# Two DFT steps joined by one SBUF-to-SBUF transfer per slot instead of a trip through a DRAM scratch, with the first chunk put in a new order

## The chip, the cores and the metric

The kernel runs on one core of a Trainium2 chip. The metric is the device time of one execution in microseconds, the median of several runs. The engines named below are PE (TensorE, matrix products), DVE (VectorE), ACT (ScalarE), POOL (GpSimd) and SP (SyncE, which here only issues DMAs). Each engine works through its own instructions in a fixed order.

## The reference

For each of 8 batches a 3136 x 256 input goes through a two-dimensional Fourier transform, of which the real part is kept. A normalised MLP with a residual follows.

```python
X = np.fft.fft(x, axis=1); X = np.fft.fft(X, axis=2); x = X.real      # x: 8 x 3136 x 256
mu = np.mean(x, axis=-1, keepdims=True)
var = np.mean((x - mu) ** 2, axis=-1, keepdims=True)
xn = (x - mu) / np.sqrt(var + 1e-06) * g_ln
ch = np.maximum(xn @ w_ch1, 0.0) @ w_ch2                              # 256 -> 1024 -> 256
return x + ch
```

The two weight matrices arrive as 64-bit floats.

## The kernel before, in words

**The transform.** The DFT of length 3136 is split into 64 x 49. `step1(b, i)` does the transforms of length 64 for batch `b` and one of 7 input tiles `i`. Each tile holds two of the 14 slots (`NS`). The result is copied by ACT into the SBUF tile `s1` (128 partitions, 14 slots, 256 values), and `step1_ends` adds the last column of each slot. `step2(m, ...)` does the second step for one of 64 pieces `m`, eight to a batch: part "m" is its matmuls, which contract over 112 partitions of `s2` (`KP`, 8 rows of each of 14 slots) with the table `tab_s`; parts "h", "f" and "l" make the high part, the full copy and the low part of the result (`ckh`, `ck`, `ckl`). The rounding into a high and a low part lets each 32-bit product be made of three faster passes.

**Between the two steps** the data must change partitions: `s1` has 128 rows per slot on the partitions, and `s2` wants 8 rows of every slot there and 16 groups in the free dimension. Before, `store1` writes two slots at a time (256 KB) into a DRAM tile `scratch`, and `relayout` reads the batch back into `s2` (1792 KB; in batch 0 in three parts, of 4, 4 and 8 groups).

**The MLP.** The 8 x 1567 spectrum rows go in 49 chunks of 256 columns. Each chunk has 8 slices of the hidden layer, so slice `s` is chunk `s // 8`. `moe1_a(s)` makes the hidden slice (PE into `ab`, ACT copies one half to `asb`, DVE adds and subtracts into `h`), `moe1_b(s)` rounds it (ACT `h_hi`, DVE `h_lo`), `moe2(s)` multiplies by the second weight into `acc`. `residual` and its followers make the residual and the statistics, `store_out` writes. The main loop runs `moe1_b(s-1)`, `moe1_a(s)`, `moe2(s-3)` for each `s` from 6 on, with the work of the later batches tied to values of `s` in two tables, `after` and `late`.

**The prologue** (batch 0, weights, first 6 slices) is an order written out by hand. The first weight comes in four pieces of 512 KB (`load_w1(n)`), each converted from 64 bits by `convert_m` (DVE, two instructions `mw`, `fw`), `convert_z` (ACT, `ew`), `convert_b` (DVE, two instructions on `ew`) and `finish_w1` (DVE, `gw`). Then `transform_w1(k, i)` transforms it on PE into `psw`, `round_w1(k)` copies the high part (`w1_hi`, ACT), `rest_w1` subtracts it on PE and `rest_w1_copy` copies the low part (`w1_lo`, ACT); `k` is the half of the hidden columns, so slices 0 to 3 need `k = 0` and slices 4 to 7 `k = 1`. The second weight goes the same way, without a transform: `load_w2(n)` puts it where `w1` piece `n` was, `convert_*`, `finish_w2` (DVE, `fw`), `split_w2` (ACT `w2_hi`, POOL `w2_lo`); piece `n` serves slices `2n` and `2n + 1`. `warm_up` are matmuls on zeros.

SP's DMAs go in the order of the code. SP and ACT share eight semaphores for their DMAs, handed out in turn, so a DMA waits until the eighth before it has landed.

Of the kernel before, what the change touches and what calls it, by code (L numbers as in the profile page):

```python
# [20 lines left out]
F32 = mybir.dt.float32  # L21
# [9 lines left out]
HALF = N // 2 + 1  # L31
# [6 lines left out]
NS = 14  # L38
# [21 lines left out]
def tables():  # L60
# [36 lines left out]
    tab = tab.transpose(3, 0, 1, 2, 4, 5).reshape(112, 2, HALF)  # L97
# [47 lines left out]
def tile_kernel(ctx: ExitStack, tc: tile.TileContext, x, g_ln, w1, w2, tu, tab, tz, ty, tw, out):  # L145
# [4 lines left out]
    dram = ctx.enter_context(tc.tile_pool(name="dram", bufs=2, space=bass.MemoryType.DRAM))  # L150
# [22 lines left out]
    def load_x(b, i):  # L173
        in_order(nc.sync.dma_start(xs[:, i], x[b, i]))

    e0c, s1, scratch, s2, zw, pieces = {}, {}, {}, {}, {}, {}
# [82 lines left out]
    def store1(b, i, eng=nc.sync):  # L259
        s = s1[b][:, 2 * i:2 * i + 2]  # L260
        in_order(eng.dma_start(scratch[b][2 * i:2 * i + 2].rearrange("s p d -> p s d"),
                               s.rearrange("p a h d -> p a (h d)")))

    def relayout(b, g0=0, g1=16, eng=nc.sync):
        if b not in s2:
            s2[b] = work.tile([128, 16, D], F32, tag="s2", name=f"s2_{b}")
        sv = scratch[b].rearrange("s (r g) d -> s r (g d)", g=16)
        in_order(eng.dma_start(s2[b][:KP, g0:g1].rearrange("r g d -> r (g d)"),
                               sv[:, :, g0 * D:g1 * D]))
# [295 lines left out]
    def w1_cols(t, k, j):  # L565
        return t[:, j, 512 * k:512 * k + 512]
# [5 lines left out]
    def rest_w1(k):  # L572

        for j in range(2):
            nc.tensor.matmul(psw[k, j], minus, w1_cols(w1_hi, k, j), start=False, stop=True,
                             skip_group_check=True)

    def rest_w1_copy(k):
        for j in range(2):
            nc.scalar.copy(w1_cols(w1_lo, k, j), psw.pop((k, j)))  # L580
# [81 lines left out]
    with tc.manual_schedule(engines={E.PE, E.Activation, E.DVE, E.Pool}):  # L662
        with tc.manual_schedule(engines={E.SP}):
# [14 lines left out]
            for i in (5, 6):  # L678
                load_x(0, i)
            load_w1(2)  # L680
            load_w1(3)
            nc.sync.dma_start(tw_all, tw)
# [12 lines left out]
            convert_b("w1_0")  # L695
            load_w2(0)
            nc.sync.dma_start(tab_s[:, :, :gb[4]], tab[:, :, :gb[4]])
            nc.sync.dma_start(tz_s, tz)
            step1_ends(0, 0, 6)
            for i in range(3):  # L700
                store1(0, i, nc.scalar if i % 2 else nc.gpsimd)
# [16 lines left out]
            load_w2(1)  # L718
            fold_zw(0, 6, nc.vector)
            step1_ends(0, 10, NS)  # L720
            store1(0, 5, nc.scalar)
            step1(0, 6)
            store1(0, 6, nc.gpsimd)
            finish_w1(1)
            convert_z("w1_3", w1p[3])
            convert_m("w1_2", w1p[2])
            convert_b("w1_2")
            finish_w1(2)
            relayout(0, 0, 4)
            relayout(0, 4, 8)  # L730
            load_w2(2)
            nc.sync.dma_start(tab_s[:, :, gb[4]:gb[8]], tab[:, :, gb[4]:gb[8]])
            relayout(0, 8, 16)
            nc.scalar.copy(minus, tw_all[:, 512:])
            transform_w1(0, 0)
            transform_w1(0, 1)
            round_w1(0)
            convert_m("w1_3", w1p[3])
            convert_b("w1_3")
            load_w2(3)  # L740
            nc.sync.dma_start(ty_s, ty)
            nc.sync.dma_start(tab_s[:, :, gb[8]:], tab[:, :, gb[8]:])
            for i in range(NU):
                load_x(1, i)
            finish_w1(3)
            transform_w1(1, 0)
            rest_w1(0)
            convert_z("w2_0", w2p[0])
            convert_z("w2_1", w2p[1])
            rest_w1_copy(0)  # L750
            transform_w1(1, 1)
            round_w1(1)
            convert_m("w2_0", w2p[0])
            convert_b("w2_0")
            f = finish_w2(0)
            split_w2(0, f)
            convert_m("w2_1", w2p[1])
            convert_b("w2_1")
            warm_up(6, warm_h)
            step2(0, "m")  # L760
            step2(0, "hl")
            step2(1, "m")
            step2(1, "hl", 0)
            f = finish_w2(1)
            moe1_a(0, ((1, 0), (0, 0), (0, 1)))
            split_w2(1, f)
            step2(0, "f")
            moe1_a(1, ((1, 0), (0, 0), (0, 1)))
            rest_w1(1)
# [64 lines left out]
```

## Time and profile before

| | |
|---|---|
| median of 3 runs | 1021.45 us (1019.89 to 1023.86) |
| the profiled execution's own time | 1021.02 us |
| its span, first to last instruction | 1019.2 us |
| busy in the span: PE, DVE, ACT, POOL | 99%, 80%, 53%, 24% |
| chain that ended last: PE, DVE, DMA | 93%, 4%, 1% |
| `scratch` writes in the chain | 5.92 us, from 22.18 us on |
| `scratch` read in the chain | 4.80 us, from 28.31 us on |
| first matmul of the second step | 33.25 us |

Times in the views below are counted from the span's start. A busy share is an average over a prologue of some 50 us, in which engines wait for each other, and a long even stretch behind it. A row of the timeline gives start, duration, engine, line, operation, tiles and, in brackets, how long the engine had been idle and what ended that. A matmul's duration includes its way through the array, so the pace of PE is read from the distance of starts.

### The profile page before, as it was taken

What the parts mean: (1) busy time and instruction counts of PE and PEld (TensorE: products, weight loads), DVE (VectorE), ACT (ScalarE), POOL (GpSimd) and SP (SyncE); (2) the same over time, 40 slices, a digit from 0 to 9 for tenths busy, and PEclk for the clock granted to TensorE, in tenths of its full rate; (3) what the DMA queues carried; (4) which work ended last, traced back from release to release, by engine and by line L of the source; (5) the groups of instructions that cost most, each with busy time, mean ns of one, the idle gap of its engine ahead of it and who ended that gap; (6) DMA issues with size and microseconds to landing.
All of it is one profiled execution on the core that took longest, in us unless ns stands there. A gap on an engine that the chain in (4) does not pass through costs nothing.

```text
span 1019.2 us, 21749 instructions
## 1 busy us (share of the span) xinstructions
PE 1005.3 (99%) x8279; PEld 984.7 (97%) x8280; DVE 813.2 (80%) x2190; ACT 540.4 (53%) x1416; POOL 244.4 (24%) x278
## 2 busy tenths in 40 slices
PE   9889999999999999999999999999999999999998
PEld 6779999999999999999999999999999999999998
DVE  7687887778787877878887887878788778878887
ACT  3545545655555455555456545555555554455453
POOL 2136504430154203341043401442024300000000
PEclk9999999999999999999999999999999999999999
DMA  9933343323222411243123132223101230100101
GB/s 348 265 129 105 105 125 104 103 74 104 74 83 94 146 52 53 85 135 104 43 89 119 66 105 81 83 94 122 56 30 46 73 104 23 42 22 22 43 22 42
DMA packets 41528, 92.10 MB, mean 90 GB/s; under 512 B 4176, under 2 KB 18704, under 8 KB 40528
## 3 DMA queue, kind: packets, MB, share of 16 engines
q1 hardware_dynamic: 40016, 88.87, 26.4%
q8 instruction: 66, 1.08, 0.4%
q0 software_dynamic: 320, 1.05, 0.3%
q10 hardware_dynamic: 1088, 0.79, 0.2%
q14 instruction: 38, 0.31, 0.1%
HBM read 50.32 MB, written 40.37 MB: 89 GB/s over the span
## 4 chain that ended last, share of the span: by engine, by line
PE 93%; DVE 4%; DMA 1%; ACT 1%; issue 0%; POOL 0%; SPq 0%; ACTq 0%; DVEq 0%
PE acc L395 52%; PE ab L345 26%; PE ps L301 5%; PE psy L419 4%; PE ps L254 3%; DVE h_lo L360 1%; PE ps L247 1%; PE ps L249 1%; DMA scratch<-s 1%; PE pw L659 1%; DVE h L351 1%; DVE h L352 1%; DMA s<-scratch 0%; ACT h_hi L359 0%; PE bb L345 0%
## 5 line engine op out<-in xcount | busy, mean ns | idle before, releaser
L395 PE MATMUL acc<-w_lo,h_hi 128*128 128x256 f32 x1568 | 438.5, 280 | 1.0 <-POOL w_lo L529 1.0
L395 PE MATMUL acc<-w_hi,h_lo 128*128 128x256 f32 x1568 | 438.5, 280 | 0.3 <-ACT w_hi L528 0.2
L395 PE MATMUL acc<-w_hi,h_hi 128*128 128x256 f32 x1568 | 438.6, 280 | 0.0
L360 DVE SCALAR_TENSOR_TENSOR h_lo<-h,h_hi 128x512 fp32r<-128x512 f32 x392 | 287.6, 734 | 173.3 <-ACT h_hi L359 171.4
L359 ACT ACTIVATE h_hi<-h 128x512 fp32r<-128x512 f32 x392 | 249.8, 637 | 259.6 <-DVE h L352 259.3
L395 PEld LDWEIGHTS acc<-w_lo,h_hi 128*128 128x128 f32 x1568 | 295.0, 188 | 1.2 <-POOL w_lo L529 1.2
L395 PEld LDWEIGHTS acc<-w_hi,h_lo 128*128 128x128 f32 x1568 | 295.3, 188 | 0.9 <-ACT w_hi L528 0.4
L395 PEld LDWEIGHTS acc<-w_hi,h_hi 128*128 128x128 f32 x1568 | 295.0, 188 | 0.0
L345 PE MATMUL ab<-ckl,w_hi 128*128 128x256 f32 x768 | 221.3, 288 | 2.3 <-DVE h L352 2.3
L345 PE MATMUL ab<-ckh,w_lo 128*128 128x256 f32 x768 | 216.7, 282 | 0.7 <-ACT w_lo L580 0.4
L345 PE MATMUL ab<-ckh,w_hi 128*128 128x256 f32 x768 | 215.5, 281 | 0.0
L217 POOL TENSOR_TENSOR fl<-f,fh 128x512 fp32r<-128x512 f32 x49 | 64.0, 1305 | 506.8 <-ACT fh L211 506.8
L351 DVE TENSOR_TENSOR h<-asb,ab 128x256 f32<-128x256 f32 x384 | 158.7, 413 | 1.9 <-ACT asb L350 1.9
L352 DVE TENSOR_TENSOR h<-asb,ab 128x256 f32<-128x256 f32 x384 | 158.7, 413 | 0.0
L345 PEld LDWEIGHTS ab<-ckl,w_hi 128*128 128x128 f32 x768 | 145.2, 189 | 6.2 <-issue 2.6
L350 ACT COPY asb<-ab 128x256 f32<-128x256 f32 x384 | 139.1, 362 | 19.8 <-PE ab L345 13.9
L345 PEld LDWEIGHTS ab<-ckh,w_lo 128*128 128x128 f32 x768 | 145.5, 189 | 3.3 <-ACT w_lo L580 0.6
L345 PEld LDWEIGHTS ab<-ckh,w_hi 128*128 128x128 f32 x768 | 145.7, 190 | 0.0
L321 ACT CAST ckh<-ps 128x392 fp32r<-128x392 f32 (+49 forms) x112 | 39.7, 356 | 66.6 <-PE ps L301 66.3
L257 ACT COPY s<-ps 128x508 f32<-128x508 f32 x56 | 32.7, 584 | 75.5 <-PE ps L254 62.5
L301 PE MATMUL ps<-tab_s,s 112*128 112x98 f32 (+1 forms) x512 | 65.6, 273 | 2.4 <-DMA s<-scratch 2.4
L301 PEld LDWEIGHTS ps<-tab_s,s 112*128 112x128 f32 x512 | 62.1, 192 | 2.9 <-issue 2.9
(108 smaller groups left out, 961.2 us busy)
## 6 DMA issues: line engine op xcount, KB each, us to landing
xs<-x SPq DMA_DIRECT2D x56, 512.0 KB, 4.3
out<-o SPq DMA_DIRECT2D x96, 256.0 KB, 2.4
scratch<-s SPq DMA_DIRECT2D x49, 256.0 KB, 2.1
s<-scratch SPq DMA_DIRECT2D x7, 1792.0 KB, 9.4
w1p_all<-w SPq DMA_DIRECT2D x8, 512.0 KB, 9.0
scratch<-s POOLq DMA_DIRECT2D x4, 256.0 KB, 6.4
s<-scratch SPq DMA_DIRECT2D x2, 448.0 KB, 5.4
s<-scratch SPq DMA_DIRECT2D x1, 896.0 KB, 12.1
```

The costliest lines, as they stand in the source:

```text
L217: nc.gpsimd.tensor_tensor(out=lo, in0=f, in1=hi.bitcast(F32), op=ALU.subtract)
L257: nc.scalar.copy(s[:, :, :, :127], ps[:, :, :, :127])
L301: nc.tensor.matmul(ps[:, h, k0 - base:k1 - base], s2[b][:KP, g, 128 * h:128 * h + 128], tab_s[:, h, k0:k1], start=(h == 0 and g == 2 * j), ...
L321: nc.scalar.copy(hi, src)
L345: nc.tensor.matmul(pt, wt[wi][:, j, fs], ch[xi][:, j, :w], start=(n == 0), stop=(n == 2))
L350: nc.scalar.copy(asb[:, :w], pa)
L351: nc.vector.tensor_tensor(out=h[:, :w], in0=asb[:, :w], in1=pb, op=ALU.add)
L352: nc.vector.tensor_tensor(out=h[:, w:], in0=asb[:, :m], in1=pb[:, :m], op=ALU.subtract)
L359: nc.scalar.activation(h_hi, h, AF.Relu)
L360: nc.vector.scalar_tensor_tensor(out=h_lo, in0=h, scalar=0.0, in1=h_hi.bitcast(F32), op0=ALU.max, op1=ALU.subtract)
L395: nc.tensor.matmul(acc[c, i][:, side], hs[xi][:, h0:h0 + 128], ws[wi][:, f], start=(f == 0 and side == 0 and n == 0), stop=(f == 7 and n = ...
L419: nc.tensor.matmul(ps[:, j, :129 + j], ck[:, j], ty_s[:, j, :129 + j], start=(j == 0), stop=True, skip_group_check=True)
```

## The change

`scratch`, `store1` and `relayout` go. `spread(b, i)` issues, for each of the two slots of tile `i`, one DMA of 128 KB from `s1` to `s2`: 128 rows of 1 KB, which become 8 partitions of 16 KB each. The rows of `tab` stand in another order to fit. `s2` is taken when `s1` is. In the later batches `spread` stands where `store1` stood. In the prologue some transfers and much of the computing move, and `rest_w1` is done half by half.

```diff
-    tab = tab.transpose(3, 0, 1, 2, 4, 5).reshape(112, 2, HALF)
+    tab = tab.reshape(112, 2, HALF)
...
-            scratch[b] = dram.tile([NS, 128, D], F32, tag="scratch", name=f"scratch{b}")
+            s2[b] = work.tile([128, 16, D], F32, tag="s2", name=f"s2_{b}")
...
-    def store1(b, i, eng=nc.sync):
...
-    def relayout(b, g0=0, g1=16, eng=nc.sync):
...
+    def spread(b, i, part=(0, 1), eng=nc.sync):
+        for s in part:
+            s += 2 * i
+            in_order(eng.dma_start(s2[b][s:KP:NS], s1[b][:, s]))
...
-            add(d0, store1, b, i)
-        add(at[-1] + 2, relayout, b)
+            add(d0, spread, b, i)
...
-            load_w1(3)
-            nc.sync.dma_start(tw_all, tw)
+            nc.sync.dma_start(tab_s[:, :, :gb[4]], tab[:, :, :gb[4]])
+            nc.sync.dma_start(tz_s, tz)
...
+            spread(0, 0, eng=nc.gpsimd)
+            spread(0, 2)
             load_w2(0)
+            load_w1(3)
...
+            spread(0, 1, eng=nc.gpsimd)
+            spread(0, 3)
+            spread(0, 4, eng=nc.gpsimd)
...
+            spread(0, 5)
             step1(0, 6)
-            store1(0, 6, nc.gpsimd)
+            spread(0, 6, (0,))
+            spread(0, 6, (1,), nc.scalar)
...
-            warm_up(6, warm_h)
...
-            moe1_a(0, ((1, 0), (0, 0), (0, 1)))
+            moe1_a(0, ((0, 0), (1, 0), (0, 1)))
...
-            convert_a("w2_3", w2p[3])
-            moe2(2)
-            add_late(6, convert_b, "w2_3")
-            add_late(7, make_w2, 3)
+            add_late(6, convert_a, "w2_3", w2p[3])
+            add_late(7, convert_b, "w2_3")
+            add_late(8, make_w2, 3)
```

The new order is shown on the engines that the prediction speaks of. The names are those of the tiles with their numbers. SP's queue from the first 22 KB table (`tz_s`) on, before: five pieces of weights and tables stand around the three reads of `scratch` (L268; the stores of batch 0 are issued by POOL and ACT).

```order
L698 DMA tz_s<-tz 112x50
L543 DMA w1p_all<-w 128x2x256
L268 DMA s_0_250<-scratch_128 112x1024 x2
L543 DMA w1p_all<-w 128x2x256
L732 DMA tab_s<-tab 112x2x392
L268 DMA s_0_250<-scratch_128 112x2048
L543 DMA w1p_all<-w 128x2x256
```

The same place now:

```order
L673 DMA tz_s<-tz 112x50
L262 DMA s_0_127<-s_0_126 8x16x256 x2
L536 DMA w1p_all<-w 128x2x256
L531 DMA w1p_all<-w 128x512
L262 DMA s_0_127<-s_0_126 8x16x256 x5
L536 DMA w1p_all<-w 128x2x256
L722 DMA tab_s<-tab 112x2x392
```

Seven of the 14 `spread` DMAs of batch 0 go by SP, behind one piece of `w2` and the last of `w1`; six go by POOL and the last by ACT.

PE between the weight transform and the first hidden slice, before (`psw_257` and `psw_259` are the half `k = 0`, `psw_283` and `psw_285` the half `k = 1`):

```order
L562 MATMUL psw_259<-gw_238,tw_all 128x512
L562 MATMUL psw_283<-gw_248,tw_all 128x512
L562 MATMUL psw_285<-gw_248,tw_all 128x512
L575 MATMUL psw_257<-w_hi,minus 128x512
L575 MATMUL psw_259<-w_hi,minus 128x512
L562 MATMUL psw_283<-gw_281,tw_all 128x512
L562 MATMUL psw_285<-gw_281,tw_all 128x512
```

There all the transforms and the subtractions of `k = 0` are done. Behind twelve rows of warming on zeros the second step follows on PE:

```order
L301 MATMUL ps_0_321<-tab_s,s_0_250 128x99 x2
L305 MATMUL ps_0_321<-tz_s,zmu 128x50
L301 MATMUL ps_0_321<-tab_s,s_0_250 128x98 x2
L301 MATMUL ps_1_332<-tab_s,s_0_250 128x98 x4
L345 MATMUL ab_343<-ckh_328,w_lo 128x256
```

The first hidden slice (`ab_343`) comes right behind it. The same place now (`psw_249`, `psw_251` are `k = 0`, `psw_332`, `psw_334` are `k = 1`):

```order
L555 MATMUL psw_251<-gw_242,tw_all 128x512
L567 MATMUL psw_249<-w_hi,minus 128x512
L294 MATMUL ps_0_276<-tab_s,s_0_127 128x99 x2
L298 MATMUL ps_0_276<-tz_s,zmu 128x50
L294 MATMUL ps_0_276<-tab_s,s_0_127 128x98 x2
L567 MATMUL psw_251<-w_hi,minus 128x512
L294 MATMUL ps_1_288<-tab_s,s_0_127 128x98 x4
L338 MATMUL ab_306<-ckh_283,w_hi 128x256
```

One subtraction now stands inside the second step. Further on, PE's rows around the third hidden slice (`ab_354`):

```order
L338 MATMUL ab_320<-ckl_284,w_hi 128x256
L555 MATMUL psw_332<-gw_255,tw_all 128x512
L555 MATMUL psw_334<-gw_255,tw_all 128x512
L338 MATMUL ab_354<-ckl_284,w_hi 128x256
```

The four transforms of the half `k = 1` and one of the two subtractions of `k = 0` have moved from ahead of the second DFT step to behind it; the transforms stand between the first hidden slices.

ACT between the high part of slice 2 and that of slice 3 now, behind `h_hi_406` (slice 2); `fw_1_373` is piece 1 of `w2`, `psw_332` and `psw_334` give the low part of `w1` for `k = 1`:

```order
L352 ACTIVATE h_hi_406<-h_362 128x512
L521 CAST w_hi<-fw_1_373 128x512
L571 CAST w_lo<-psw_332 128x512
L571 CAST w_lo<-psw_334 128x512
L352 ACTIVATE h_hi_431<-h_402 128x512
```

Before, `w_hi` of that piece stood ahead of the first high part, and the two casts behind the high part of slice 2 and the `asb` of slice 3. What ACT does there now waits first for `fw_1_373` from DVE.

DVE up to the last piece of `w2` (`fw_3`), before:

```order
L524 SCALAR_TENSOR_TENSOR ew_3_499<-w1p_all,ew_3_499 128x512
L360 SCALAR_TENSOR_TENSOR h_lo_555<-h_530,h_hi_554 128x512
L351 TENSOR_TENSOR h_566<-asb_565,ab_558 128x256
L352 TENSOR_TENSOR h_566<-asb_565,ab_558 128x256
L584 SCALAR_TENSOR_TENSOR fw_3_501<-fw_3_501,ew_3_499 128x512
```

and now:

```order
L517 SCALAR_TENSOR_TENSOR ew_3_522<-w1p_all,ew_3_522 128x512
L353 SCALAR_TENSOR_TENSOR h_lo_583<-h_558,h_hi_582 128x512
L344 TENSOR_TENSOR h_594<-asb_593,ab_586 128x256
L345 TENSOR_TENSOR h_594<-asb_593,ab_586 128x256
L426 TENSOR_TENSOR y_0_598<-ye_0_562,psy_0_540 128x129
L427 TENSOR_TENSOR y_0_598<-ye_0_562,psy_0_540 128x128
L434 BN_STATS st_0_602<-y_0_598 128x6
L435 BN_AGGR mv_601<-st_0_602 128x2
L575 SCALAR_TENSOR_TENSOR fw_3_524<-fw_3_524,ew_3_522 128x512
```

Before, `h_566` is slice 7; now `h_594` is slice 8. The last step for this piece stands one slice later, and behind a tile of the residual.

More of the change, by code (lines that the diff above doesn't have):

```diff
@@ L174, in load_x @@
         in_order(nc.sync.dma_start(xs[:, i], x[b, i]))
-    e0c, s1, scratch, s2, zw, pieces = {}, {}, {}, {}, {}, {}
+    e0c, s1, s2, zw, pieces = {}, {}, {}, {}, {}
     def ends(b, p0=0, p1=NS, eng=nc.gpsimd):
@@ L570, in round_w1, with rest_w1, rest_w1_copy @@
             nc.scalar.copy(w1_cols(w1_hi, k, j), psw[k, j])
[L572 to L580, printed above, removed]
+    def rest_w1(k, j):
+        nc.tensor.matmul(psw[k, j], minus, w1_cols(w1_hi, k, j), start=False, stop=True,
+                         skip_group_check=True)
+    def rest_w1_copy(k, j):
+        nc.scalar.copy(w1_cols(w1_lo, k, j), psw.pop((k, j)))
     def finish_w2(n):
@@ L695, in tile_kernel @@
             convert_b("w1_0")
+            step1_ends(0, 0, 6)
+            spread(0, 0, eng=nc.gpsimd)
+            spread(0, 2)
             load_w2(0)
[L697 to L701, printed above, removed]
+            load_w1(3)
             ends(0, 6, 10)
@@ L717, in tile_kernel @@
             convert_b("w1_1")
-            load_w2(1)
             fold_zw(0, 6, nc.vector)
             step1_ends(0, 10, NS)
-            store1(0, 5, nc.scalar)
+            spread(0, 5)
             step1(0, 6)
-            store1(0, 6, nc.gpsimd)
+            spread(0, 6, (0,))
+            spread(0, 6, (1,), nc.scalar)
             finish_w1(1)
-            convert_z("w1_3", w1p[3])
+            nc.scalar.copy(minus, tw_all[:, 512:])
             convert_m("w1_2", w1p[2])
+            transform_w1(0, 0)
@@ L727, in tile_kernel @@
             convert_b("w1_2")
             finish_w1(2)
-            relayout(0, 0, 4)
-            relayout(0, 4, 8)
+            load_w2(1)
+            nc.sync.dma_start(tab_s[:, :, gb[4]:gb[8]], tab[:, :, gb[4]:gb[8]])
             load_w2(2)
[L732 to L735, printed above, removed]
+            nc.sync.dma_start(ty_s, ty)
+            nc.sync.dma_start(tab_s[:, :, gb[8]:], tab[:, :, gb[8]:])
@@ L739, in tile_kernel @@
+            split_w2(0, f0)
+            moe1_a(1, ((0, 0), (1, 0), (0, 1)))
+            transform_w1(1, 0)
             convert_b("w1_3")
+            moe1_b(0)
+            finish_w1(3)
             load_w2(3)
-            nc.sync.dma_start(ty_s, ty)
-            nc.sync.dma_start(tab_s[:, :, gb[8]:], tab[:, :, gb[8]:])
             for i in range(NU):
                 load_x(1, i)
[L745 to L748, printed above, removed]
+            step2(0, "f")
@@ L749, in tile_kernel @@
+            moe1_a(2)
+            moe1_b(1)
             convert_z("w2_1", w2p[1])
-            rest_w1_copy(0)
+            convert_m("w2_1", w2p[1])
+            moe2(0)
             transform_w1(1, 1)
             round_w1(1)
[L753 to L757, printed above, removed]
-            convert_b("w2_1")
-            warm_up(6, warm_h)
-            step2(0, "m")
-            step2(0, "hl")
@@ L779, in tile_kernel @@
-            moe2(0)
-            moe1_b(3)
-            moe1_a(4)
-            convert_b("w2_2")
-            f = finish_w2(2)
-            split_w2(2, f)
+            moe1_a(3)
+            moe1_b(2)
+            convert_b("w2_1")
+            f1 = finish_w2(1)
+            moe2(1)
+            rest_w1(1, 0)
+            rest_w1(1, 1)
+            split_w2(1, f1)
+            rest_w1_copy(1, 0)
+            rest_w1_copy(1, 1)
+            moe1_b(3)
+            step2(1, "hl", 1)
+            convert_a("w2_2", w2p[2])
@@ L785, in tile_kernel @@
+            moe1_a(4)
+            step2(1, "f")
+            moe2(2)
+            step2(2, "m")
+            moe1_b(4)
+            convert_b("w2_2")
+            f2 = finish_w2(2)
+            step2(2, "h")
+            moe1_a(5)
+            split_w2(2, f2)
+            step2(2, "l")
+            step2(2, "f")
             nc.gpsimd.tensor_scalar(out=neg, in0=ty_s[:, 1, 129:130], scalar1=2.0, scalar2=-1.0,
                                     op0=ALU.mult, op1=ALU.add)
-            moe2(1)
-            step2(2, "m")
```

45 lines of the change are left out of this document (15 added, 30 removed).

## Prediction

> **What bounds the kernel now.** I read the page first, then the windows by stage, the chain of waits, and PE's timeline of the first chunk. The page:
>
> ```profile
> span 1019.2 us, 21749 instructions
> PE 1005.3 (99%) x8279; PEld 984.7 (97%) x8280; DVE 813.2 (80%) x2190; ACT 540.4 (53%) x1416; POOL 244.4 (24%) x278
> ```
>
> PE is the bound by its share, but a share is a mean. The windows tell where anything can be won (columns: stretch, length, busy time of PE, PEld, DVE, ACT, POOL with counts, granted clock, DMA share, GB/s):
>
> ```profile
> 10.00:20.00 10.00, 10.00 (x54) 8.62 (x53) 9.29 (x22) 4.69 (x12) 3.87 (x7) 1.00 1.03 413
> 20.00:27.00 7.00, 6.34 (x19) 3.15 (x18) 5.78 (x11) 3.09 (x6) 0.75 (x1) 1.00 1.05 388
> 112.00:1000.00 888.00, 888.00 (x7488) 882.15 (x7487) 713.20 (x1953) 479.12 (x1262) 201.62 (x223) 1.00 0.23 76
> ```
>
> From 112 to 1000 us PE is busy for 888.00 of 888.00 us: there the batches' transfers are hidden already, and a shorter way between the steps wins nothing. From 10 to 27 us the DMA engines are full. So the case is decided before 112 us. The chain of waits there (start, length, what):
>
> ```profile
> 21.30 0.59 ACT s L257
> ...
> 22.18 5.92 DMA scratch<-s
> ...
> 28.31 4.80 DMA s<-scratch
> 33.11 0.14 issue
> 33.25 0.66 PE ps L301 x4
> ...
> 35.82 2.92 PE ab L345 x12
> 38.74 0.77 PE psw L575 x2
> 39.51 0.72 PE ab L345 x6
> ```
>
> The last copy out of the first step ends at 21.9; then two transfers follow one another, the write to scratch and the read back, and the second step starts at 33.25. The reader should also see that 12 matmuls take 2.92 us at 35.82, and 6 of them 0.72 at 39.51, where 12 would take 1.44: PE ran at half pace after its idle time, and lost some 1.5 us.
>
> **The sum is made against the profiled execution**, 1021.02 us (span 1019.2 and 1.8 around it). The median of the runs is 1021.45, 0.4 above, well inside their spread. Call S the start of the second step, 33.25 before.
>
> **One transfer for two.** The read back (4.80 us and some 0.3 of issue) leaves the chain. What remains is when the last `spread` lands. How long a transfer out of `s1` takes is shown from both sides, first under the prologue's load, then in the later batches:
>
> ```profile
> DMA to landing us min/median/max: 5.1/6.6/8.2
> DMA to landing us min/median/max: 2.1/2.1/4.0
> ```
>
> With a last issue between 21.9 and 22.5, it lands between 24.0 and 30.7. I take the place where the last write to scratch lands before, 22.18 + 5.92 = 28.1. The queues say why. Ahead of that write stand tables (`tw_all`, the first part of `tab_s`, `tz_s`), three pieces of weight (two of `w1`, one of `w2`) and 1792 KB of `s1`; ahead of the last `spread` stand the same, only in another order, and the engines are full at 413 and 388 GB/s. So S = 28.1 + 0.14 = 28.25, 5.0 earlier. From below S is bounded by PE itself, by these rows (timeline: start, length, records; two records are one of these matmuls):
>
> ```profile
> 26.78 1.03 PE L575 MATMUL psw<-w_hi,minus 128*128 128x512 f32 x2
> 27.65 1.88 PE L562 MATMUL psw<-gw,tw_all 128*128 128x512 f32 x4
> 29.58 1.24 PE L659 MATMUL pw<-warm_h 128*128 128x512 bf16 x5
> 33.25 0.66 PE L301 MATMUL ps<-tab_s,s 112*128 112x99 f32 x4 [2.43 <-DMA s<-scratch]
> ```
>
> A transform matmul keeps PE for 0.86 us (two in 1.88 with the array's delay), a subtraction for 0.40. Four transforms from 21.3 on end at 24.7, the rounding (0.6) and one subtraction end at 25.7. So S lies between 25.7 and 30.8.
>
> **Work that loses its cover.** Before, the four transforms and two subtractions around 23 to 29.5 us ran while the data travelled. Four transforms (half `k = 1`) and one subtraction now stand behind S: 4 x 0.86 + 0.40 = 3.84 us of PE, all on the path, since PE is the bound there. The removed warming (1.24 us at 29.58) lay in the wait, and counts nothing. Its cover gone, it could have cost the clock; but PE now idles from about 25.7 to 28.25, as long as the 2.43 before, so I expect one slow stretch again, price 0, ends -1.5 and +1.5.
>
> **New waits in the first chunk.** DVE's pace is read from start to start:
>
> ```profile
> 52.09 0.41 DVE L509 TENSOR_SCALAR mw<-w1p_all 128x512 int32<-128x512 int32 x1
> 52.60 0.69 DVE L511 SCALAR_TENSOR_TENSOR fw<-w1p_all,mw 128x512 f32<-128x512 uint32 x1
> 53.21 0.68 DVE L360 SCALAR_TENSOR_TENSOR h_lo<-h,h_hi 128x512 fp32r<-128x512 f32 x1
> ...
> 54.48 0.42 DVE L522 TENSOR_SCALAR ew<-ew 128x512 int32<-128x512 int32 x1
> 54.93 0.69 DVE L524 SCALAR_TENSOR_TENSOR ew<-w1p_all,ew 128x512 int32<-128x512 int32 x1
> 55.54 0.69 DVE L360 SCALAR_TENSOR_TENSOR h_lo<-h,h_hi 128x512 fp32r<-128x512 f32 x1
> 56.14 0.41 DVE L351 TENSOR_TENSOR h<-asb,ab 128x256 f32<-128x256 f32 x1
> ...
> 56.80 0.68 DVE L584 SCALAR_TENSOR_TENSOR fw<-fw,ew 128x512 f32<-128x512 f32 x1
> ...
> 60.62 0.28 DVE L433 TENSOR_TENSOR y<-ye,psy 128x129 f32<-128x129 f32 x1
> ...
> 61.69 0.29 DVE L529 TENSOR_TENSOR t_lo<-tu_s,t_hi 128x128 fp32r<-128x128 f32 x1
> ```
>
> So `mw` and `fw` take 1.12, the two `ew` 1.06, `h_lo` 0.60, both halves of `h` 0.66, the closing `fw` 0.68, one residual tile 1.07. ACT's means:
>
> ```profile
> L350 ACT COPY asb<-ab 128x256 f32<-128x256 f32 x9 | 3.3, 367 | 2.4 <-PE ab L345 2.4
> L528 ACT CAST w_hi<-fw 128x512 fp32r<-128x512 f32 x3 | 1.9, 621 | 4.1 <-DVE fw L584 4.1
> L580 ACT CAST w_lo<-psw 128x512 fp32r<-128x512 f32 x2 | 1.1, 592 | 0.0
> ```
>
> And what PE waited for at this place before:
>
> ```profile
> 42.93 0.39 PE L345 MATMUL ab<-ckh,w_lo 128*128 128x256 f32 x1 [0.37 <-ACT w_lo L580]
> ...
> 51.77 0.36 PE L345 MATMUL ab<-ckl,w_hi 128*128 128x256 f32 x1 [0.44 <-DVE h L352]
> ...
> 54.70 0.36 PE L345 MATMUL ab<-ckl,w_hi 128*128 128x256 f32 x1 [0.57 <-DVE h L352]
> ...
> 58.20 0.38 PE L395 MATMUL acc<-w_hi,h_lo 128*128 128x256 f32 x1 [0.21 <-ACT w_hi L528]
> 59.54 0.39 PE L395 MATMUL acc<-w_lo,h_hi 128*128 128x256 f32 x1 [0.97 <-POOL w_lo L529]
> ...
> 63.39 0.36 PE L345 MATMUL ab<-ckl,w_hi 128*128 128x256 f32 x1 [0.20 <-DVE h L352]
> 66.00 0.35 PE L345 MATMUL ab<-ckl,w_hi 128*128 128x256 f32 x1 [0.24 <-DVE h L352]
> 73.10 0.71 PE L419 MATMUL psy<-ty_s,ck 128*128 128x129 f32 x4 [1.31 <-DVE o L470]
> ```
>
> - *`moe2(0)`* needs `h_lo` of slice 0. From the first low part `ckl` on, DVE now does the closing `fw` of `w2` piece 0 (0.68), `mw` and `fw` of the late `w1` piece 3 (1.12), `h` twice (1.32), two `ew` (1.06) and `h_lo` (0.7): 4.9. PE has the rest of slices 0 and 1 (1.2), two transforms (1.72) and slice 2 (0.72): 3.6. It waits 1.2 with a handover; before, not at all.
> - *`moe1_a(4)`* needs the low part of `w1`, `k = 1`. On ACT that cast stands behind `w_hi` of `w2` piece 1, which waits for DVE. From the end of slice 3 on PE: `asb` 0.37, `h` 0.75, `h_lo` 0.60, `ew` 1.06, `fw` 0.68, `w_hi` 0.62, `w_lo` 0.59, together 4.7. PE has `moe2(1)` (1.44), two subtractions (0.80) and one matmul (0.12). Wait 2.3. Behind the blocked cast ACT also holds slice 3's high part, so DVE idles too. A wait of 0.37 for the same cast stood there before, so 1.9 are new.
> - *`moe2(6)`* needs `w2` piece 3. Before it waited 0.21 + 0.97. Its closing `fw` now stands one `h_lo` (0.60), one `h` (0.66) and one residual tile (1.07) later: 2.3 more.
>
> Together 5.4, with ends 0 (DVE gets ahead in the 5 us won) and 8 (waits add up in the queues). **Given back:** the waits at 51.77 and 54.70 were for DVE in the midst of conversions that now stand elsewhere (1.0), and of the later 0.20, 0.24 and 1.31 half, since DVE catches up while PE stands (0.9); ends 0 and 3.
>
> **Rest.** Each later batch issues 14 DMAs on SP where there were 8. What hides them is the even stretch from 112 us on, where PE waits for no transfer, and the data now arrive a transfer earlier; price 0. Were that cover gone, each batch's second step would wait. POOL issues six transfers for four in the prologue, the last four behind all its sums `e0c`, so nothing waits for POOL longer than before. Removed DRAM traffic after 112 us is hidden traffic. `tab`'s order is made on the host.
>
> **Sum:** -5.0 + 3.84 + 5.4 - 1.9 = +2.3, so 1023.3 us. In general: 1021.0 + S - 25.9. A microsecond of landing is a microsecond of time.
>
> [...] In the rows above a write of 256 KB with 128 rows lands in 2.1 us when the engines are free. [...]
>
> **Rivals.**
> - *Half of the engines carry the spreads*, because one side of each has only 8 rows. Eight of the 14 go by SP and ACT, 1.05 MB. On 8 engines that is 65.5 KB more for each, at 413/16 = 25.8 GB/s 2.5 us. S = 30.75, time 1025.9. For it: that shape, and that the engines are full until 27 us, so nothing hides the longer queue. Against it: no transfer here shows fewer engines at work. [...]
> - *Slower: DVE becomes the bound of the first chunk.* Behind S stand now the whole of `w1` piece 3 (1.12 + 1.06 + 0.7), the closing `fw` of `w2` piece 0 (0.68) and the conversion of piece 1 (2.2), 5.8 us that DVE did in its idle time before S. If DVE paces PE up to `moe2(6)`, the change is 5.8 - 5.0 = +0.8 plus every us that DVE idles more than before there. It decides from 4.3 us more; the blocked ACT queue at slice 3 and the late PE at slice 2 and 3 give about 5 by the same rows: +5.8, 1026.8. Against it: before, no wait of PE for DVE in these slices was longer than 0.57.
> - *Faster: the data land before PE is ready.* S = 25.9, so no idle time, no slow clock (-1.5), and DVE starts 7.3 earlier, so that only the wait at `moe2(6)` arises: -7.3 + 3.84 - 1.5 + 2.3 - 1.9 = -4.6; with half of that last wait, -5.8 and 1015.3. For it: transfers of 2.1 us. Against it: full DMA engines to 27 us.
> - *Early landing with the waits:* S = 26.2 gives 1021.3, no change.
>
> **Chances.** The forecast 0.40 (its own range 1021 to 1026), early landing 0.12, half of the engines 0.15 (a third of it over the bound), slower by DVE 0.15, faster 0.18. About 0.5%, 5.1 us, is what a measurement of this kernel can tell from no change. Hence faster 0.18, within 0.62, slower 0.20. The range 1016 to 1028 leaves out the tail of the fast case and waits beyond 8.
>
> **What would show it.** In the changed profile: the second step's first matmul at 28.25, waiting for a spread; PE without idle time from 112 on; waits at the first `acc` for `h_lo`, at `ab` of slice 4 for the `w_lo` cast, and at `acc` of slice 6 for `w_lo` of piece 3, together 6 to 7 us; one slow stretch of PE. Wrong it is if S lies below 26 or above 31, if those waits are under 3 us, or if PE waits in later batches.

## The result, and the profile after

| | before | changed |
|---|---|---|
| median of 6 runs | 1022.38 us (1019.89 to 1023.86) | 1035.55 us (1034.96 to 1036.45) |
| ratio to before | 1 | 1.0132, 95% interval 1.0118 to 1.0145 |
| the profiled execution's own time | 1021.02 us | 1036.45 us |
| S, start of the second step | 33.25 us | 37.44 us |

The changed kernel is 1.3% slower, some 13 us. The page and the windows of the changed kernel, as they stood of before (stretch, length, PE, PEld, DVE, ACT, POOL, granted clock, DMA share, GB/s):

```profile
span 1034.7 us, 21806 instructions
PE 1009.5 (98%) x8274; PEld 989.0 (96%) x8274; DVE 812.1 (78%) x2190; ACT 542.7 (52%) x1416; POOL 246.3 (24%) x280
```

```profile
10.00:20.00 10.00, 10.00 (x54) 8.94 (x53) 8.49 (x20) 4.35 (x10) 4.93 (x10) 1.00 1.05 373
20.00:27.00 7.00, 5.70 (x20) 3.07 (x19) 2.62 (x5) 2.01 (x6) 0.00 (x0) 1.00 1.06 219
112.00:1000.00 888.00, 887.12 (x7466) 880.17 (x7465) 711.12 (x1947) 479.80 (x1257) 211.90 (x231) 1.00 0.20 63
18.00:28.00 10.00, 7.70 (x30) 4.86 (x30) 4.62 (x9) 2.49 (x8) 1.58 (x3) 1.00 1.04 217
28.00:33.00 5.00, 0.79 (x1) 0.29 (x1) 2.15 (x4) 2.21 (x4) 0.00 (x0) 0.51 0.53 157
```

The last two stretches in the kernel before:

```profile
18.00:28.00 10.00, 9.34 (x33) 5.29 (x32) 8.38 (x15) 4.36 (x10) 1.65 (x4) 1.00 0.97 362
28.00:33.00 5.00, 2.77 (x9) 0.97 (x8) 2.85 (x6) 3.14 (x6) 0.36 (x1) 1.00 0.74 193
```

From 112 us on little happened: PE waits three times for `h`, at 119 to 125 us, 0.9 us together. new_order_scratch below has the same three waits and no_spread0 has none, so they are the tail of a late first chunk and not a price of the later batches. The row to look at is 20 to 27 us: the DMA engines are as full as before (1.06), yet they move 219 GB/s where they moved 388. From 28 to 33 us half of them work on average (0.53; 0.55 from 31.3 to 33, when only packets of spreads by SP and ACT begin), and PE does nearly nothing, at half clock (0.51). PE's rows at S and the chain (start, length, what):

```profile
30.50 0.79 PE L567 MATMUL psw<-w_hi,minus 128*128 128x512 f32 x1 [4.80 <-ACT w_hi L563]
37.44 1.15 PE L294 MATMUL ps<-tab_s,s 112*128 112x99 f32 x4 [6.14 <-DMA w1p_all<-w]
```

```profile
22.22 0.59 ACT s L256
...
22.84 9.06 DMA s<-s
...
31.96 5.49 DMA w1p_all<-w
37.45 1.13 PE ps L294 x4
```

The releaser at 37.44 is named wrongly: the second step does not read `w1p_all`, and that load's own 16 semaphore increments end at 38.96. The reason is that a `spread` by SP or ACT leaves only nine increments in the trace, one about 1.1 us after its issue and eight when data land, where every other DMA leaves 16, so that the profile gives no landing for these spreads. Counted by hand on each semaphore, the last two spreads, issued at 23.07 and 25.46, landed at 35.70 and 36.73. That is what S waited for. The last one also went out late. SP issued the last five of its spreads in this stretch (start, length, count):

```profile
19.26 6.82 SPq L262 DMA_DIRECT2D s<-s  x5
```

The fifth had to wait for the semaphore of the spread issued eight DMAs before it, at 15.25, which landed at 25.40.

PE's waits in the changed kernel (total, times, longest; the first is the one just corrected):

```profile
PE ps L294 <- DMA w1p_all<-w: 6.1, 1, 6.1
PE psw L567 <- ACT w_hi L563: 4.8, 1, 4.8
PE acc L388 <- ACT w_hi L521: 3.6, 1, 3.6
PE ab L338 <- ACT w_lo L571: 2.8, 1, 2.8
PE acc L388 <- POOL w_lo L522: 1.0, 1, 1.0
PE ab L338 <- DVE h L345: 0.9, 3, 0.3
PE acc L388 <- ACT asb L343: 0.5, 1, 0.5
```

The wait for `w_hi` at 30.50 lies inside the wait for the data: ACT's rounding stood behind the conversion of `w2` piece 0, whose load was slow as well (issued 16.58, landed 29.22).

### The profile page after: what moved, and what is told of

It reads as the page before. It is cut to its first block, busy times and chain, and to the rows that moved or that the text cites. A ratio compares the mean times of both kernels' runs of the same rounds, so it can differ in the third digit from the quotient of the medians.

```text
span 1034.7 us, 21806 instructions
## 1 busy us (share of the span) xinstructions
PE 1009.5 (98%) x8274; PEld 989.0 (96%) x8274; DVE 812.1 (78%) x2190; ACT 542.7 (52%) x1416; POOL 246.3 (24%) x280
## 4 chain that ended last, share of the span: by engine, by line
PE 92%; DVE 3%; DMA 1%; issue 1%; ACT 1%; POOL 0%; ACTq 0%; POOLq 0%; SPq 0%
PE acc L388 51%; PE ab L338 26%; PE ps L294 6%; PE psy L412 4%; PE ps L253 3%; DMA s<-s 1%; DVE h_lo L353 1%; PE pw L649 1%; PE ps L246 1%; PE ps L248 1%; DMA w1p_all<-w 1%; DVE h L344 0%; DVE h L345 0%; ACT h_hi L352 0%; PE psw L555 0%
## 5 line engine op out<-in xcount | busy, mean ns | idle before, releaser
L353 DVE SCALAR_TENSOR_TENSOR h_lo<-h,h_hi 128x512 fp32r<-128x512 f32 x392 | 284.6, 726 | 176.0 <-ACT h_hi L352 174.1
L343 ACT COPY asb<-ab 128x256 f32<-128x256 f32 x384 | 139.6, 363 | 23.9 <-PE ab L338 18.1
L294 PE MATMUL ps<-tab_s,s 112*128 112x98 f32 (+1 forms) x512 | 68.4, 280 | 6.1 <-DMA w1p_all<-w 6.1
L294 PEld LDWEIGHTS ps<-tab_s,s 112*128 112x128 f32 x512 | 64.9, 198 | 6.7 <-issue 6.6
```

What stands on the lines that cost most here:

```text
L294: nc.tensor.matmul(ps[:, h, k0 - base:k1 - base], s2[b][:KP, g, 128 * h:128 * h + 128], tab_s[:, h, k0:k1], start=(h == 0 and g == 2 * j), ...
L343: nc.scalar.copy(asb[:, :w], pa)
L353: nc.vector.scalar_tensor_tensor(out=h_lo, in0=h, scalar=0.0, in1=h_hi.bitcast(F32), op0=ALU.max, op1=ALU.subtract)
```

## The experiments

In the table, each run's trace columns come from one profiled execution; "landed" is the last landing of a spread of batch 0, counted from the semaphore increments; "packet" is the mean time of POOL's 4 KB packets of batch 0's spreads in the trace's DMA records; "half clock" is the time at half clock up to 1000 us; "rate" is the window 18 to 28 us. A ratio is to executions of before that were timed in the same session as the run, so it can differ from the quotient of two times in the table. The changed kernel and warmed issue the same DMAs in the same order, and their last landings differ by 2.1 us, so smaller differences of a landing prove nothing by themselves. "Formula" is 1021.0 + S - 25.9 from the prediction.

| run | S | landed | rate GB/s | packet ns | half clock us | time us | formula | ratio (95%) |
|---|---|---|---|---|---|---|---|---|
| before | 33.25 | - | 362 | - | 3.4 | 1022.38 | - | 1 |
| changed | 37.44 | 36.73 | 217 | 316 | 23.9 | 1035.55 | 1032.5 | 1.0132 (1.0118-1.0145) |
| no_spread0 | 25.58 | - | 326 | - | 6.8 | 1021.63 | 1020.7 | 0.9995 (0.9982-1.0008) |
| new_order_scratch | 31.46 | - | 319 | - | 23.9 | 1031.89 | 1026.6 | 1.0097 (1.0073-1.0121) |
| old_order_spread | 41.33 | 40.56 | 246 | 282 | 6.8 | 1027.74 | - | 1.0056 (1.0035-1.0076) |
| later_only | 33.00 | - | 358 | - | 3.4 | 1023.27 | - | 1.0006 (0.9988-1.0023) |
| sixteen_rows | 28.64 | 30.11 | 279 | 235 | 20.5 | 1028.88 | 1023.7 | 1.0056 (1.0037-1.0075) |
| straight | 25.32 | 27.97 | 341 | 188 | 10.2 | 1022.60 | 1020.4 | 0.9998 (0.9987-1.0009) |
| all_pool | 36.94 | 36.48 | 242 | 271 | 27.3 | 1038.21 | 1032.0 | 1.0153 (1.0130-1.0176) |
| warmed | 36.49 | 34.62 | 219 | 320 | 3.4 | 1032.82 | 1031.6 | 1.0104 (1.0079-1.0130) |
| all_sp | 37.32 | 37.08 | 218 | - | 27.3 | 1038.42 | 1032.4 | 1.0157 (1.0131-1.0183) |
| neighbours | 49.48 | 48.81 | 152 | 547 | 41.0 | 1049.64 | 1044.6 | 1.0272 (1.0246-1.0299) |
| sp_only | 36.98 | 36.74 | 206 | - | 23.9 | 1037.37 | 1032.1 | 1.0138 (1.0122-1.0155) |
| apart | 34.69 | 34.02 | 228 | 272 | 23.9 | 1034.75 | 1029.8 | 1.0117 (1.0098-1.0135) |
| before_two_groups | 31.86 | - | 354 | - | 0 | 1019.14 | - | 0.9973 (0.9958-0.9988) |
| before_two_groups_warm | 32.38 | - | 358 | - | 0 | 1019.57 | - | 0.9972 (0.9961-0.9983) |

### Is it the landing, or the order?

**no_spread0**

```diff
+            alloc1(0)
+            nc.gpsimd.memset(s2[0], 0.0)
...
         for s in part:
-            s += 2 * i
-            in_order(eng.dma_start(s2[b][s:KP:NS], s1[b][:, s]))
+            s += 2 * i
+            if b:
+                in_order(eng.dma_start(s2[b][s:KP:NS], s1[b][:, s]))
```

> The changed kernel, but in batch 0 no spread is issued; s2 of batch 0 is zeroed by POOL at the start instead, so the first 392 rows of tables meet zeros (part of the computation is left out). All else stands as in the changed kernel. Theory 1 (the late landing of the spreads is the cause: S, the start of the second step, is 37.44 us and every microsecond of it is time): S falls to where the first subtraction waits for the rounded weight, 26 to 29 us, and the time to 1020 to 1026 us. Rival (the new order of the first chunk costs it, whatever the transfers do): the time stays above 1030 us although S falls.

PE's row at S:

```profile
25.58 0.58 PE L295 MATMUL ps<-tab_s,s 112*128 112x99 f32 x4
```

S fell to 25.58, a little below the range given, and the time to 1021.63, 0.9 above the formula: the theory stands. (Without the spreads the loads come earlier too: the first subtraction, which in the changed kernel stood behind one until 30.50, begins at 25.24. straight, below, keeps the traffic, and has S at 25.32 and 1022.60 us.) It says more. With S 7.7 us ahead of before, the new order is no faster than the old one, so what the order itself costs is some 7 us.

**new_order_scratch**

```diff
-            spread(0, 0, eng=nc.gpsimd)
-            spread(0, 2)
+            store1(0, 0, nc.gpsimd)
+            store1(0, 1, nc.scalar)
+            store1(0, 2, nc.gpsimd)
...
+            relayout(0, 0, 4)
+            relayout(0, 4, 8)
+            relayout(0, 8, 16)
```

> The changed kernel's order in the prologue and the first chunk, but with the scratch: store1 where the spreads stand (on POOL and ACT in turn, as before), three relayout parts behind them on SP, in all batches. Theory 1 (spreads land late): S comes to 32 to 34 us, where two transfers in a row put it before, against 37.44 with the spreads, and the time to 1021.0 + 33.25 - 25.9 = 1028.4, range 1026 to 1031. Rival (the order alone): S may fall, but the time stays at 1034 to 1037 us.

```profile
31.46 1.18 PE L301 MATMUL ps<-tab_s,s 112*128 112x99 f32 x4 [5.67 <-DMA s<-scratch]
```

S fell as expected (a little more), but the time, 1031.89, lies above the range given. Two transfers through DRAM beat one from SBUF to SBUF by 6 us at S. The last write to `scratch`, issued at 22.55, landed at 26.54, with the same loads ahead of it as the spreads have. But the order under it is 9.5 us slower than before although S is 1.8 earlier. Some 5 us of this the formula does not know; the section on the clock says what they probably are.

**old_order_spread.** The old order with spreads in place of `store1`, two for each tile on the queue that had the write, and no `relayout`:

```diff
-            for i in range(3):
-                store1(0, i, nc.scalar if i % 2 else nc.gpsimd)
+            for i in range(3):
+                spread(0, i, nc.scalar if i % 2 else nc.gpsimd)
```

> The kernel before, in its own order, with spreads in place of store1 (same engines: POOL and ACT in turn) and no relayout, in all batches. Theory 1 (spreads land late): S is 34 to 38 us instead of 33.25, and the time 1022 to 1027 us, since the four transforms stay ahead of S and the waits of the new order do not arise. Rival (the order alone; a spread is one transfer and lands by 28 to 30): S is 29 to 31 us and the time 1017 to 1020 us.

S came at 41.33, later than either theory said, for another reason. ACT's timeline:

```profile
22.04 8.00 ACTq L260 DMA_DIRECT2D s<-s  x2
30.08 0.58 ACT L256 COPY s<-ps 128x508 f32<-128x508 f32 x1 [8.72 <-DMA tab_s<-tab]
```

Twice as many DMAs use up the eight semaphores that SP and ACT share. Of the 8 us of this row ACT stood 6.8 ahead of the second spread, until a table load eight DMAs back had landed (29.39), and the last copy out of the first step stood behind it. So the run does not tell the theories apart; it shows what a DMA issued by an engine with other work can cost. The old order, with more work ahead of S, lost only 5 us by an S 8 us later.

**later_only.** The kernel before, with single SBUF-to-SBUF DMAs in the batches from 1 on:

```diff
-            add(d0, store1, b, i)
-        add(at[-1] + 2, relayout, b)
+            add(d0, spread, b, i)
```

> The kernel before with its scratch, relayout and order in batch 0; only the batches from 1 on go by one SBUF-to-SBUF DMA for each slot (into 8 neighbouring partitions of s2, the layout that the kernel before has). Theory 1 and the prediction's price 0 for the later batches: 1020 to 1024 us, no difference from before, PE without idle time from 112 us on. Rival (105 more issues on SP or slower spreads cost something in the even stretch): 1025 us or more.

```profile
112.00:1000.00 888.00, 888.00 (x7489) 882.17 (x7488) 710.50 (x1953) 479.38 (x1262) 200.27 (x223) 1.00 0.26 63
```

No difference (1.0006, 0.9988 to 1.0023) and PE without a gap. The change of the later batches is free, and wins nothing.

### Why the spreads land late

All seven kernels here are the changed kernel with one thing about batch 0's spreads altered.

**sixteen_rows** and **straight**: the destination has 16 or 128 partitions instead of 8.

```diff
-            in_order(eng.dma_start(s2[b][s:KP:NS], s1[b][:, s]))
+            d = s2[b][s % 7:KP:7, 8 * (s // 7):8 * (s // 7) + 8] if b == 0 else s2[b][s:KP:NS]  # sixteen_rows
+            d = s2[b][:, s] if b == 0 else s2[b][s:KP:NS]                                       # straight
+            in_order(eng.dma_start(d, s1[b][:, s]))
```

> The changed kernel, but in batch 0 each spread (same queue, same place, same 128 KB) goes to 16 partitions x 8 groups instead of 8 partitions x 16 groups, so that both sides have 16 rows (the data of batch 0 come to the wrong places, so the result of that batch is not the transform). Theory A (a spread by SP or ACT runs on 8 of the 16 DMA engines): the DMA share between 28 and 33 us goes from 0.53 towards 1, S from 37.4 to 33 to 35.5 us, and the time to 1030 to 1034 us. Theory B (packets are slow because few partitions are written at once): S falls further, to 30 to 33 us. Rival C (any SBUF-to-SBUF transfer is that slow among the loads): S stays at 36 to 38 us and the time at 1034 to 1036.

> The changed kernel, but in batch 0 each spread is a straight copy of the same 128 KB from the 128 partitions of s1 to the same 128 partitions of s2 (the data of batch 0 come to the wrong places; the last two groups of s2 are zeroed by POOL at the start). [...] Theory A (8 of 16 engines): as with 16 rows, S 33 to 35.5 us. Theory B (few partitions written at once): S 28 to 31 us, clearly below the run with 16 rows, and the time 1023 to 1029 us. Rival C (SBUF-to-SBUF in itself): S 36 to 38 us.

The windows of the first, then of the second:

```profile
18.00:28.00 10.00, 6.98 (x26) 3.98 (x24) 5.63 (x10) 4.49 (x10) 1.64 (x4) 1.00 1.07 279
```

```profile
18.00:28.00 10.00, 9.08 (x45) 6.14 (x43) 6.11 (x11) 5.73 (x14) 1.57 (x3) 1.00 1.07 341
```

In both kernels the first piece of the second step reads two groups that only some of the slots fill, so S may lie ahead of the last landing; the landings are what to compare: 36.73, 30.11 and 27.97 us for 8, 16 and 128 partitions. Queues, bytes and sources are the same. Theory C is out, since a straight SBUF-to-SBUF copy lands at 27.97, the 28.1 of the prediction. Theory A alone is out too: both have 16 rows or more, yet packets into 128 partitions take 188 ns and with 16 partitions 235, at 341 and 279 GB/s (their landings, 2.1 us apart, would not be enough to say so).

**all_pool**, **all_sp** and **sp_only** were meant to try the two causes one by one.

```diff
-            spread(0, 2)                       # all_pool; so for every spread of batch 0
+            spread(0, 2, eng=nc.gpsimd)
...
-            spread(0, 0, eng=nc.gpsimd)        # all_sp; so for the six on POOL
+            spread(0, 0)
...
-            spread(0, 6, (1,), nc.scalar)      # sp_only: all_sp and this
+            spread(0, 6, (1,))
```

> The changed kernel with all 14 spreads of batch 0 issued by POOL, whose spreads post 16 landings and not 8. Theory A: the half of the engines is gone, the last issue comes at 23 to 25 us and lands 8 to 10 us later as POOL's six do now: S 32 to 35 us, time 1029 to 1034. Theory B or C: POOL's packets of 4 KB took 0.32 us instead of 0.16, and all 14 are then so slow: S 36 to 40 us, time 1034 to 1039.

POOL's spreads post 16 increments, and yet the last landing is at 36.48, as late as ever. The increments don't say that 16 engines carry a spread: in this trace the 32 packets of the first spread run at most eight at a time, where the first 32 in straight reach 13. So the half of the engines is not clearly gone here. But successive spreads overlap (12 packets at a time in the first 64), and from 18 to 28 us the 16 engines are full (1.07) and carry 242 GB/s; a 4 KB packet takes 271 ns. So no engines stand idle, and the packets are slow. POOL too had to wait for landings eight spreads back, 4.8 us in all, so that its last spread went out at 27.65.

> The changed kernel with none of batch 0's spreads on POOL: the six go by SP at the same places, so SP issues 13 and ACT one. Theory A (8 of 16 engines): six more spreads on the same eight engines, 6 x 0.74 us (16 packets of 1 KB at 46 ns for each engine) later: S 40 to 42 us, time 1037 to 1041. [...]

SP's queue (start, length, count) and the window behind it:

```profile
19.89 12.99 SPq L262 DMA_DIRECT2D s<-s  x9
```

```profile
28.00:33.00 5.00, 0.00 (x0) 0.00 (x0) 0.00 (x0) 0.00 (x0) 0.00 (x0) 0.81 0.36 108
```

SP stood between its issues at 20.55 and 28.21 for the landing of ACT's single spread, whose semaphore it needed, so S says nothing of the theories. The packets say a little: 2 KB packets that begin between 18 and 33 us took 116 ns where the changed kernel has 144. But the engines were less busy with SP standing (share 0.75 from 18 to 28 us, against 1.04), so part of that may be the lighter load.

> The changed kernel with all 14 spreads of batch 0 on SP, the last one too that stood on ACT, so that SP no longer waits from 20.55 to 28.21 us for a landing of ACT's. Theory (packets of SP's spreads are near full speed, 46 ns for 1 KB, and only the half of the engines is left as a cause): a spread lands some 1.1 us behind the one ahead, as the first ones did in the run before (20.2, 21.3, 22.4, 23.7), the last at 30 to 32 us; S 30.5 to 32.5 us, time 1026 to 1031. Rival (8 engines alone make it as late as it is now): S 36 us or more, time 1035 or more.

Without that stall the last spread still landed at 36.74, and the theory's 30 to 32 was wrong. The window:

```profile
28.00:33.00 5.00, 0.00 (x0) 0.00 (x0) 0.22 (x1) 0.39 (x1) 0.00 (x0) 0.52 0.79 218
```

From the fifth on the spreads landed one behind the other, 0.6 to 1.3 us apart, beside the loads (share 0.79 in the window); and each issue waited for the landing eight DMAs back, so the last went out at 28.76. The premise that these packets go at full speed failed, too: between 18 and 33 us a 1 KB packet took 65 ns, against 46 in the writes to `scratch` before, and a 2 KB packet 121, against 88. So neither all_pool nor sp_only has one cause without the other. What is shown is the two together: with straight copies the last landing is 27.97, with 8 partitions 36.73 (34.62 in warmed, below). How the 7 to 9 us divide between the half of the engines and the slow packets stays open. In the changed kernel itself the two show one after the other: 1 KB packets that begin between 18 and 28 us, beside the loads and POOL's spreads, took 82 ns, and those between 28 and 33, mostly alone and with half of the engines at work (0.53), 51.

**neighbours** and **apart** leave engines, queues, bytes and packet sizes alone, and move only the partitions.

```diff
-            in_order(eng.dma_start(s2[b][s:KP:NS], s1[b][:, s]))
+            in_order(eng.dma_start(s2[b][8 * s:8 * s + 8], s1[b][:, s]))     # neighbours
+            in_order(eng.dma_start(s2[b][APART[s]:KP:NS], s1[b][:, s]))      # apart: 0, 7, 1, 8, 2, 9, ...
```

> The changed kernel with the layout of s2 that the kernel before has: the 8 rows of a slot go to 8 neighbouring partitions instead of to every 14th (and the tables' rows stand to match). Theory B1 (only the number of partitions written counts): S 36 to 38.5 us and the time 1034 to 1037, as in the changed kernel. Theory B2 (neighbouring partitions share a way in): the packets get slower still, S 39 us or more, time 1038 or more.

```profile
18.00:28.00 10.00, 7.53 (x30) 4.71 (x28) 4.44 (x9) 2.33 (x8) 1.33 (x3) 0.99 1.10 152
```

```profile
DMA to landing us min/median/max: 9.5/14.6/17.5
```

The second fence is the view of POOL's spreads; in the changed kernel the same row reads:

```profile
DMA to landing us min/median/max: 7.7/10.4/11.6
```

> The changed kernel with the slots in another order in s2: successive spreads write rows 7 partitions apart (slot 2i to row i, slot 2i+1 to row i+7 of each 14), where they are neighbours now; the tables' rows stand to match. Queues, engines and bytes are the same. Theory B2 (partitions near each other share a way in, so transfers in flight at once get in each other's way): POOL's packets of 4 KB fall from 316 ns to 230 to 290, S to 32 to 36 us, time to 1028 to 1034. Rival B1 (only the number of partitions of one transfer counts): S 36.5 to 38.5 us, time 1034 to 1037.

What B2 expected came, clearly in one direction: with 8 neighbouring partitions a 4 KB packet takes 547 ns, the last landing is 12 us later and S is 49.48. Number of engines, queues and bytes are those of the changed kernel, so slow packets by themselves can move the landing that far. With successive spreads 7 partitions apart it takes 272, against 316 and 320 in the two runs with the changed layout. The landing, 34.02, is below both of theirs (36.73 and 34.62), but not by more than they differ, and the intervals of the times overlap. The time, 1034.75, lies above B2's range. So the packets got faster; that the kernel did is not shown, nor that neighbours share a way in.

### The clock

**warmed**

```diff
             transform_w1(0, 1)
+            warm_up(20, warm_h)
...
             rest_w1_copy(0, 0)
+            warm_up(26, warm_h)
             step2(0, "m")
```

> The changed kernel with matmuls on zeros where PE waits: 20 ahead of the first subtraction and 26 ahead of the second step (0.216 us each at full speed, 4.3 and 5.6 us against waits of 4.8 and 6.1). Theory (the granted clock falls because PE idles; it is half from 28.13 to 45.20 us and costs some 4 to 5 us beside the landing): S stays within 1 us of 37.4, the granted clock stays at 1.00 until 45 us and the time falls to 1029 to 1032 us. Rival (the slow clock has no part in the 13 us, or comes anyway): 1034 to 1037 us.

The same stretch, changed kernel first, then warmed:

```profile
28.00:45.00 17.00, 8.01 (x32) 7.19 (x33) 5.19 (x11) 4.99 (x10) 0.00 (x0) 0.50 0.74 189
```

```profile
28.00:45.00 17.00, 15.37 (x82) 9.28 (x81) 8.34 (x18) 7.67 (x17) 1.28 (x1) 1.00 0.66 190
```

The clock stayed at 1.00, and the time fell by 2.7 us, to just above the range. (The intervals of the two ratios overlap, but every time of warmed, 1033.55 at most, is below every one of the changed kernel, 1034.96 at least.) S gives 0.9 of it. It is set here by the warming itself, which ran over the landing at 34.62:

```profile
30.64 5.79 PE L649 MATMUL pw<-warm_h 128*128 128x512 bf16 x26
36.49 0.69 PE L294 MATMUL ps<-tab_s,s 112*128 112x99 f32 x4
```

The other 1.8 are the clock's by this account (2.8, if the two profiled executions are compared), after what a faster PE gives back in waits for DVE (`h` 1.7 instead of 0.9, `h_lo` 0.8 instead of 0.2). So PE's idle time cost twice here: itself, and the half clock that followed (23.9 us of it, against 3.4 in warmed). In the table the formula is short by 0.9 and 1.2 us where at most 6.8 us ran at half clock, by 3.0 to 6.2 where 20 to 41 did. That holds for new_order_scratch as well; only for the changed kernel was it tested by warming.

### A version that beats both

**before_two_groups** and, with warming, **before_two_groups_warm**:

```diff
-            relayout(0, 0, 4)
-            relayout(0, 4, 8)
+            relayout(0, 0, 2)
+            relayout(0, 2, 4)
+            relayout(0, 4, 8)
...
-            warm_up(6, warm_h)
+            warm_up(14, warm_h)                # the second kernel only
```

> The kernel before with the first read of scratch cut in two (2 groups of the 16 and 2, instead of 4 at once), since the first piece of the second step needs two groups. If a microsecond of landing is a microsecond of time there too, S goes from 33.25 to 32.3 to 32.8 us and the time falls by 0.5 to 1 us. Rival (a read of half the size lands no earlier among the loads): no change.

> As the run before, and 14 warming matmuls instead of 6 ahead of the second step (8 x 0.216 = 1.7 us more, inside the wait of 2.4). Theory (PE's idle time there brings the slow clock, 35.86 to 39.27 us before): the granted clock stays at 1.00, and the time is 1.5 to 2.5 us under the kernel before. Rival: the clock falls anyway, time 0 to 1 us under before.

PE at S in the first, and the window that held before's slow stretch:

```profile
31.86 0.66 PE L301 MATMUL ps<-tab_s,s 112*128 112x99 f32 x4 [1.05 <-DMA s<-scratch]
```

```profile
33.00:38.00 5.00, 4.32 (x30) 3.53 (x29) 2.62 (x7) 2.89 (x9) 2.37 (x2) 1.00 1.02 263
```

The first read lands 1.4 us earlier, PE idles 1.05 us instead of 2.43, and in the profiled execution the slow stretch does not come. The time is 0.9973 of before (0.9958 to 0.9988), 2.8 us, more than the 0.5 to 1 expected. The clock was not in that expectation: 1.4 us of landing and the 1.5 us that before lost at half pace would make 2.9. More warming adds nothing to the median (0.9972): it kept PE until 32.32 and the second step began at 32.38. It makes the time steadier, though. The 12 executions without it had a mean clock of 0.996 to 1.000 and took 1017.9 to 1022.5 us; with it they had 0.999 to 1.000 and took 1019.3 to 1020.5.

## Why the prediction was wrong, point by point

The forecast was 1023.3 us (1016 to 1028), the measured time 1035.55.

- **The step that failed: when the last spread lands.** The prediction put it at 28.1, where the last write to `scratch` landed, by the argument that the same bytes stand ahead of it and the engines are full. They were full at 219 GB/s, not at 388. The argument holds for a transfer that writes all partitions (straight: 27.97) and for the scratch (new_order_scratch: 26.54); a spread writes 8. The last issue, put between 21.9 and 22.5, came at 25.46, because it needed a semaphore that an earlier late spread still held, and it landed 11.3 us later. S was 37.44 instead of 28.25, outside the bound of 30.8, because that bound came from writes to DRAM, which showed neither cause.
- **The rival "half of the engines"** had its mechanism right (DMA share 0.53, eight landings) and its size wrong: 2.5 us were priced, from the bytes at full packet speed, and its 1025.9 was still 10 us short. How much it makes by itself no run shows: in sp_only, where the landing is 8.6 us later than the prediction's, the packets were slow as well. No rival had the slow packets.
- **Work without cover, 3.84:** borne out as part of a balance, not measured alone. In no_spread0 the rows give S -7.67, +3.84 and waits of about +5, a sum of +1.1, where the runs gave -0.5 with some 1.3 either way: a little too much, and not separable from the waits.
- **New waits, 5.4, given back 1.9:** at `moe1_a(4)` 2.8 (2.3 forecast), at `moe2(6)` 3.6 + 1.0 (3.5), at `moe2(0)` 0.5 (1.2). Less the 0.37 and 1.18 that stood there before, 6.3 are new. Given back are 1.4 at `h` and the 1.3 at `o`, 2.7. The net is 3.6, forecast 3.5; that it is so close is partly luck, since single terms are off by up to 1.1.
- **The clock, price 0:** wrong. PE idled 10.9 us ahead of S, not about 2.4; half clock lasted 17.07 us there and 3.41 twice later, against 3.41 in all before.
- **Rest, 0:** right (later_only). The 0.9 us of waits at 119 to 125 us, which the prediction had as a sign of being wrong, come from the late first chunk.
- **The sum** with the measured terms: S +4.2, cover +3.8, waits +3.6 make 11.6 of the 15.4 us between the two profiled executions. The 3.8 left are put down to the clock, of which the warming accounts for some 1.8; the rest is argued, not shown.

Each part of the change was a loss here except the later batches, where it cost and won nothing. The new order breaks even with before at about S = 25.6 (no_spread0, and straight at 25.32), and no run with a later S did.

## What to carry to other kernels

Before one DMA replaces two, look at the side with fewest rows: here each transfer wrote 8 partitions, which went with half of the DMA engines (share 0.53, eight landings) and with slow packets (316 ns for 4 KB, where 128 partitions had 188), and the loads beside it paid as well (2 KB packets took 144 ns, where straight had 95). Which 8 partitions they were mattered, too (547 ns with 8 neighbours). A DMA share near 1 didn't say that the engines moved much (1.06 at 219 GB/s, 1.05 at 388 before): read GB/s beside it. And an order that moves work behind a wait bets on the wait's end, so price it with the late end too, the slow clock included.

## What the runs showed of the hardware

- **Packets into few partitions were slow, those of the loads beside them too.** A 4 KB packet took 188 ns into 128 partitions, 235 with 16, 316 and 320 with 8 (every 14th) and 547 with 8 neighbours; 2 KB packets (most are of weight loads) that begin between 18 and 33 us took 95, 104, 144 and 249. The rates from 18 to 28 us have the same order: 341, 279, 217 and 152 GB/s. With the two spreads of a tile 7 partitions apart (apart) a 4 KB packet took 272 ns, at 228 GB/s. Why the partitions matter no run shows, and the prediction did not reckon with it.
- **Sixteen increments didn't mean sixteen packets at a time:** POOL's spreads post 16, but the first one in all_pool ran its 32 packets at most eight at a time.
- **With less traffic beside it, a spread was quick:** in the first later batch of the changed kernel the eight landings come 2.4 to 4.0 us after the issue, at a DMA share of 0.35 (97 to 146 us). The last two spreads of batch 0, at 0.99 (23 to 28 us) and then 0.53, landed 12.6 and 11.3 us after theirs.
- **Half clock came in steps of 3.41 us** (17.07 in the changed kernel is five of them; 6.83 in old_order_spread, 10.24 in sixteen_rows and 13.65 in new_order_scratch are two, three and four) after idle time of PE, and did not come after 1.05 us of it in the one execution profiled (before_two_groups).
